# First input rows loaded whole instead of as even and odd halves, with the opening order that goes with it

## The chip, the cores and the metric

The kernel runs on one core of a Trainium2 chip. The metric is the time of one execution on the device in microseconds (us), the median of several runs. The kernel is written against the engines themselves: TensorE (PE in the profile) multiplies, VectorE (DVE) and ScalarE (ACT) do elementwise work and empty the accumulators, GpSimd (POOL) does little, and SyncE (SP) issues nearly all the DMA transfers.

## What is computed

Two convolutions of five taps with stride two over time, each with a gelu, and then a joint of every time step with eight label vectors:

```python
# x (2, 4000, 512), w1, w2 (5, 512, 512), g (2, 8, 512), w_f, w_g, w_o (512, 512), all bf16
h = zeros_like(x)
for i in range(5):
    h = h + einsum("btc,cd->btd", pad(x)[:, i:i+T, :], w1[i])
h = gelu(h)[:, ::2, :]                       # 2000 steps
f = zeros_like(h)
for i in range(5):
    f = f + einsum("btc,cd->btd", pad(h)[:, i:i+T1, :], w2[i])
f = gelu(f)[:, ::2, :]                       # 1000 steps
fe = einsum("btd,de->bte", f, w_f)
ge = einsum("bud,de->bue", g, w_g)
j = tanh(fe[:, :, None, :] + ge[:, None, :, :])
return einsum("btud,dv->btuv", j, w_o)       # (2, 1000, 8, 512)
```

## The kernel before: what the change touches

The program is first written down as a list of operations with what they read and write. A list scheduler with a simple model of durations then fixes the order of the operations of each engine; TensorE and SyncE keep the written order where they are pinned, VectorE, ScalarE and GpSimd are reordered by it. Semaphore waits are derived from that order. So a small edit at the start can change the order of the other engines far behind it.

The convolutions are computed by phases of time (row number modulo 4), with sums and differences of inputs and of weights in place of some of the products. The first tile of `x` (1024 rows, in two blocks of 512 called xr0 and xr1) is loaded with rows in the partitions and transposed by TensorE against an identity; all later tiles come through transposing DMAs. The even rows of a group of four are phases 0 and 2, the odd rows 1 and 3. Here each block is loaded in two transfers, even rows first:

```python
        def load_xr(rt, pp):
            dst = xr[rt][pp::2].map(lambda a: a.rearrange("p r k c -> p r (k c)"))
            src = x[1, 4 * P * rt:4 * P * (rt + 1), :].rearrange("(p r) c -> p r c", r=4)[:, pp::2, :]
            return pl.dma("sp", lambda e: e.dma_start(dst.ap, src), (), (dst,), nbytes=262144)
...
        came = [load_xr(rt, 0) for rt in range(2)]
        act(warm[0:1], warm[1:2], ACT.Gelu_apprx_tanh)
        # w1[i], 512 KB each; `after`: issued when the named earlier transfer has landed
        def load_w1(i, after=None):
            o = load_w("sp", w1_sb[i], w1[i].rearrange("(k c) d -> c k d", c=P))
            if after is not None:
                o.after.append(after.idx)
            return o

        came.append(load_w1(0))
        came += [load_xr(rt, 1) for rt in range(2)]
        for i in (4, 1, 3, 2):
            came.append(load_w1(i, came[-3]))
        for ph in (2, 3, 1, 0):
            load_x(0, ph, 272, 528)
```

`came[-3]` is the third last transfer issued so far: it holds each weight back until an earlier transfer has landed.

TensorE first multiplies zeros (`NWARM = 7` matmuls of 512 columns) while nothing has arrived. Then `turn(pp)` transposes the even (`pp` 0) or odd (`pp` 1) rows of both blocks and copies them from the accumulator into `xs[0]`:

```python
        def warm_mm(n):
            z, zz = zero[0:P], zero[:]
            for i in range(n):
                o = ps.cols((3, 1)[i % 2] * NT, NT)
                mm(o, [(z, zz)], True, True)

        warm_mm(NWARM)
        psb = ps.h[:, :].bitcast(BF16)
        def turn(pp):
            for rt in range(2):
                bk = (1, 3)[rt] if pp else 4 + rt
                pv = View(psb[:, bk * 1024:(bk + 1) * 1024].rearrange("p (r k c) -> p r k c", r=2, k=NK), np.array([bk]), True)

                def fn(e, rt=rt, pv=pv):
                    for r in range(2):
                        for k in range(NK):
                            ins = e.transpose(pv.ap[:, r, k, :], xr[rt].h[:, 2 * r + pp, k, :], ident.h[:, :])
                    return ins
                pl.op("pe", fn, (xr[rt][pp::2], ident[:]), (pv,), 0.6)
                o = xs[0][pp::2, :, 16 + rt * P:16 + (rt + 1) * P]
                if rt:
                    act(o, pv, ACT.Copy)
                else:
                    pl.op("dve", lambda e, o=o, pv=pv: e.tensor_copy(out=o.ap, in_=pv.ap), (pv,), (o,), vec_cost(o, (pv,)))

```

The opening order. `direct(i)` is tap i for the first 128 output channels (8 products of 252 columns); `filt3(w)` is one combined tap for the three other channel groups (12 products). `t0.shift` (ScalarE) and `t0.xf` (VectorE) make the sums and differences of inputs, `w1sum13` and `w1sums` (VectorE, with halvings on ScalarE) those of weights, into `w1_t`, called w_t in the profile:

```python
        turn(0)
        t0.xf("a0")
        t0.shift("a3")
        t0.xf("a3")
        direct(0)
        filt3("a0")
        turn(1)
        t0.shift("b1")
        for w in ("b1", "b3", "a1", "a2"):
            t0.xf(w)
        w1sum13()
        w1sums(2, "s")
        w1sums(1, "s")
        direct(4)
        filt3("a3")
        direct(1)
        direct(3)
        filt3("b1", "b3")
        direct(2)
        pl.pin = ("pe",)

...     # inputs of the second tile; the "+" and "-" halves of the weight sums
        filt3("b2")
        for m in base0:
            filt(m, "a1", "a2")
        t0.gelu(0, ps.pair(0, 256, NA))
```

The tap 2 weight is also halved in place by ScalarE (`w1_sb[2]`, within `w1sum13`), and later in the program the difference `w_b = w1[1] - w1[3]` is made by VectorE and scaled by ScalarE. It is needed much later, and the scheduler decides where it stands.

Of the kernel before, what the change touches and what calls it, by code (L numbers as in the profile page):

```python
# [11 lines left out]
P = 128  # L12
# [297 lines left out]
def bass_standalone__seq2seq_rnn_t_joint__speech_kernel(  # L310
# [30 lines left out]
    NSLOT = 12  # L341
    BU = B * U
    NT = 512
    NWARM = 7
    START = (0, 334, 667, 1000)

    with ExitStack() as es:
        BASE = 16512

        def at(name, shape, dtype, offset):  # L350
            return Buf(nc, name, shape, dtype, BASE + offset)
# [12 lines left out]
        xr = [at(f"xr{i}", [4, NK, P], BF16, H[1] + i * 4096) for i in range(2)]  # L364
# [13 lines left out]
        ident = at("ident", [P], BF16, small + 1408)  # L378
# [13 lines left out]
        pl = Plan(nc)  # L392
# [3 lines left out]
        def vec_cost(o, ins, fast=True):  # L396
            bf = fast and all(not v.psum and v.ap.dtype == BF16 for v in (o,) + tuple(ins))
            return o.ap.free_size() * (0.52e-3 if bf else 1.04e-3) + 0.065
# [8 lines left out]
        def act(o, i, func, scale=1.0, bias=None, cost=None):  # L407
            rd = (i,) if bias is None else (i, bias)
            pl.op("act", lambda e: e.activation(o.ap, i.ap, func, scale=scale,  # L409
                                                bias=0.0 if bias is None else bias.ap), rd, (o,),  # L410
                  cost or o.ap.free_size() * 0.83e-3 + 0.13)

        def mm(o, pairs, start, stop, check=True):

            def fn(e):
                for n, (l, r) in enumerate(pairs):
                    ins = e.matmul(o.ap, lhsT=l.ap, rhs=r.ap, start=start and n == 0,  # L417
                                   stop=stop and n == len(pairs) - 1, skip_group_check=not check)
                return ins
            pl.op("pe", fn, [v for pr in pairs for v in pr], (o,), len(pairs) * max(o.ap.free_size() / 2400 + 0.0025, 0.1))  # L420
# [13 lines left out]
        def load_w(eng, dst, src):  # L434
            return pl.dma(eng, lambda e: e.dma_start(dst.ap, src), (), (dst,))

        def load_xr(rt, pp):
            dst = xr[rt][pp::2].map(lambda a: a.rearrange("p r k c -> p r (k c)"))
            src = x[1, 4 * P * rt:4 * P * (rt + 1), :].rearrange("(p r) c -> p r c", r=4)[:, pp::2, :]
            return pl.dma("sp", lambda e: e.dma_start(dst.ap, src), (), (dst,), nbytes=262144)  # L440

        def load_x(s, ph, lo, hi):

# [4 lines left out]
            pl.dma("sp", lambda e: e.dma_start_transpose(out=dst.ap, in_=src), (), (dst,),  # L448
                   nbytes=(hi - lo) * D * 2, rate=180e3)

        came = [load_xr(rt, 0) for rt in range(2)]
        act(warm[0:1], warm[1:2], ACT.Gelu_apprx_tanh)

        def load_w1(i, after=None):
# [3 lines that stand above are left out]
            return o  # L458

        came.append(load_w1(0))  # L460
        came += [load_xr(rt, 1) for rt in range(2)]
        for i in (4, 1, 3, 2):
            came.append(load_w1(i, came[-3]))
        for ph in (2, 3, 1, 0):
            load_x(0, ph, 272, 528)
# [29 lines left out]
# [5 lines that stand above are left out]

        warm_mm(NWARM)
        psb = ps.h[:, :].bitcast(BF16)
        def turn(pp):
            for rt in range(2):
                bk = (1, 3)[rt] if pp else 4 + rt
                pv = View(psb[:, bk * 1024:(bk + 1) * 1024].rearrange("p (r k c) -> p r k c", r=2, k=NK), np.array([bk]), True)

                def fn(e, rt=rt, pv=pv):
                    for r in range(2):
                        for k in range(NK):  # L510
                            ins = e.transpose(pv.ap[:, r, k, :], xr[rt].h[:, 2 * r + pp, k, :], ident.h[:, :])
                    return ins
                pl.op("pe", fn, (xr[rt][pp::2], ident[:]), (pv,), 0.6)
                o = xs[0][pp::2, :, 16 + rt * P:16 + (rt + 1) * P]
                if rt:
                    act(o, pv, ACT.Copy)
                else:
                    pl.op("dve", lambda e, o=o, pv=pv: e.tensor_copy(out=o.ap, in_=pv.ap), (pv,), (o,), vec_cost(o, (pv,)))

        def shift(src, off, dst, c0, n, which):  # L520

            r, d, kind = {"a0": (2, -1, 0), "a3": (0, 1, 2), "b1": (3, -1, 3)}[which]
            act(dst[kind, :, c0:c0 + n], src[r, :, off + d:off + d + n], ACT.Copy)
# [47 lines left out]
        def w1sums(m, part):  # L571


            nm = 2 if m == 2 else 1
            sl = slice(m * P, (m + nm) * P)
            s = ws[m][:]
            if part == "s":
                tt("dve", s, w1_sb[0, :, sl], w1_sb[4, :, sl], add)
            elif part == "+":
                stt("dve", w1_t[2, :, sl], s, 0.5, w1_sb[2, :, sl], add)  # L580
            else:
                stt("dve", w1_t[0, :, sl], s, 0.5, w1_sb[2, :, sl], sub)
# [286 lines left out]
        t0, t1 = tiles[0:2]  # L869
# [3 lines left out]
        def direct(i):  # L873
            for m in (0,):
                for s in range(2):
                    r, d = tap_at[i][s]
                    mm(ps.cols(m * NT + 256 * s, NA),
                       [(w1_sb[i, k, m * P:(m + 1) * P], xs[0][r, k, 16 + d:16 + d + NA]) for k in range(NK)],
                       i == 0 and s == 0, i == 2, False)
# [3 lines left out]
        def filt(m, *which):  # L883
            A = base0[m]
            C = A + NT
            for w in which:
                o = {"a0": A, "b1": A, "b3": A + NA, "a3": A + NA, "b2": C, "a1": C, "a2": C + NA}[w]
                t0.product(w, m, o, w in ("a0", "b2"))

        def filt3(*which):  # L890
            for w in which:
                for m in base0:
                    filt(m, w)

        turn(0)
        t0.xf("a0")
        t0.shift("a3")
        t0.xf("a3")
        direct(0)
        filt3("a0")  # L900
        turn(1)
        t0.shift("b1")
        for w in ("b1", "b3", "a1", "a2"):
            t0.xf(w)
        w1sum13()
        w1sums(2, "s")
        w1sums(1, "s")
        direct(4)
        filt3("a3")
        direct(1)  # L910
        direct(3)
        filt3("b1", "b3")
        direct(2)
        pl.pin = ("pe",)

# [225 lines left out]
```

## Time and profile before

| | us |
|---|---|
| median of 3 runs | 272.36 |
| lowest and highest | 271.94, 273.29 |
| span of the profiled run | 270.1 |
| TensorE busy | 261.5 |
| VectorE busy | 200.9 |
| ScalarE busy | 181.1 |

The profile is of one execution. Each engine's busy time is the time in which it had an instruction running; a weight load of TensorE (PEld) lies beside the products and is counted apart. In a timeline each line is a run of like instructions: start and duration in us, engine, source line, operation, the tile written and the tile read, the count, and in brackets the idle time of the engine ahead of it with what ended it. The lines named L404, L409 and L417 are helpers that record every elementwise operation of VectorE, every activation and every matmul, so a group is told by its tiles, not by its line. L511 is the transposes, L518 a copy out of the accumulator, L585 a scalar-tensor-tensor operation of VectorE.

The transfers of the program, of which those into xr and w_sb matter here, by size and median time from issue to landing:

| transfer | count | KB each | us to landing |
|---|---|---|---|
| xr from x | 4 | 256 | 4.8 |
| w_sb from w1 and w2 | 10 | 512 | 5.7 |
| xs from x, transposing | 8 | | 4.7 |

### The profile page before, as it was taken

The numbers are of one execution on the slowest core, as the hardware profiler recorded it, in microseconds if no ns is written. First come the engines' busy times: TensorE is split into PE (matmuls) and PEld (weight loads), VectorE is DVE, ScalarE is ACT, GpSimd is POOL, SyncE is SP. The second block draws the span as 40 slices with busy tenths as digits, with TensorE's granted clock in tenths as the row PEclk, the third lists the DMA queues.
The fourth block names the chain that finished last, engine by engine and source line by source line (L and its number), as shares of the span: only waits on it lengthen the run. The fifth ranks groups of instructions, "written<-read, shape, count | busy, mean of one in ns | idle before, by whom it ended". The sixth has DMA issues, their size and how long they took to land.

```text
span 270.1 us, 4333 instructions
## 1 busy us (share of the span) xinstructions
PE 261.5 (97%) x1579; PEld 152.7 (57%) x1579; DVE 200.9 (74%) x362; ACT 181.1 (67%) x302; POOL 6.8 (3%) x20
## 2 busy tenths in 40 slices
PE   6898999999999999999999999999999999999995
PEld 3696765446666556666566545555665444444442
DVE  1389999999999999996233999844345667656664
ACT  2356989995365999667636668738447695959720
POOL 1000003210000000000000000000000000000000
PEclk9799999999999999999999999999999999999999
DMA  5799992969996022111111113321101353454444
GB/s 174 265 239 213 277 283 55 205 117 189 252 177 123 2 78 78 61 38 61 61 39 58 61 59 108 130 77 58 61 19 59 130 164 117 159 190 157 146 148 135
DMA packets 57506, 33.91 MB, mean 126 GB/s; under 512 B 31614, under 2 KB 57486, under 8 KB 57486
## 3 DMA queue, kind: packets, MB, share of 16 engines
q1 hardware_dynamic: 55230, 31.49, 42.9%
q0 software_dynamic: 2112, 2.10, 4.5%
q8 instruction: 12, 0.20, 0.3%
q14 instruction: 8, 0.07, 0.1%
q10 hardware_dynamic: 144, 0.07, 0.1%
HBM read 7.86 MB, written 16.38 MB: 90 GB/s over the span
## 4 chain that ended last, share of the span: by engine, by line
PE 87%; DMA 5%; DVE 3%; ACT 2%; issue 1%; SPq 0%; ACTq 0%
PE acc L417 87%; DMA w_sb<-in_w_dram 5%; ACT jT L409 1%; DVE w_t L585 1%; DVE feT L985 1%; DVE ws L404 1%; SPq L440 0%; DVE zx L404 0%; DVE w_t L404 0%; ACT w_sb L409 0%; DVE row L734 0%; ACT feT L409 0%; ACT fT L409 0%; ACT ost L409 0%; ACTq L271 0%
## 5 line engine op out<-in xcount | busy, mean ns | idle before, releaser
L417 PE MATMUL acc<-wo_sb,jT 128*128 128x512 bf16 (+1 forms) x504 | 114.9, 377 | 0.7 <-ACT jT L409 0.7
L1033 DVE CAST ost<-acc 128x512 bf16<-128x512 f32 (+1 forms) x95 | 64.8, 686 | 37.7 <-PE acc L417 37.7
L409 ACT ACTIVATE jT<-feT,geT 128x1000 bf16<-128x1000 f32 (+16 forms) x100 | 76.6, 820 | 13.3 <-PE acc L417 10.2
L417 PEld LDWEIGHTS acc<-wo_sb,jT 128*128 128x128 bf16 x504 | 49.2, 98 | 53.5 <-ACT jT L409 1.0
L409 ACT ACTIVATE ost<-acc 128x512 bf16<-128x512 f32 (+1 forms) x31 | 18.1, 583 | 16.4 <-PE acc L417 16.0
L417 PE MATMUL acc<-xt,w_sb 128*128 128x252 bf16 (+1 forms) x144 | 24.6, 317 | 0.0
L409 ACT ACTIVATE sd<-acc 128x334 f32<-128x334 f32 (+1 forms) x32 | 13.9, 445 | 11.0 <-PE acc L417 10.9
L409 ACT ACTIVATE hT<-acc 128x334 bf16<-128x334 f32 (+3 forms) x33 | 15.1, 466 | 8.1 <-PE acc L417 7.9
L417 PE MATMUL acc<-row,w_sb 128*128 128x334 bf16 (+1 forms) x112 | 20.5, 305 | 0.0
L417 PEld LDWEIGHTS acc<-xt,w_sb 128*128 128x128 bf16 x144 | 14.6, 102 | 7.5 <-DVE xt L404 0.3
L417 PE MATMUL acc<-zx,w_sb 128*128 128x334 bf16 (+1 forms) x96 | 17.6, 305 | 0.0
L404 DVE TENSOR_TENSOR sd<-sd 128x334 f32<-128x334 f32 (+1 forms) x16 | 8.0, 502 | 10.4 <-ACT sd L409 10.3
L417 PE MATMUL acc<-row,w_t 128*128 128x334 bf16 (+1 forms) x80 | 14.6, 305 | 0.0
L417 PE MATMUL acc<-xs,w_t 128*128 128x252 bf16 (+1 forms) x76 | 14.0, 314 | 0.4 <-issue 0.4
L417 PEld LDWEIGHTS acc<-row,w_sb 128*128 128x128 bf16 x112 | 10.9, 98 | 6.1
L417 PE MATMUL acc<-fT,wf_sb 128*128 128x333 bf16 (+1 forms) x96 | 14.0, 305 | 0.2 <-ACT fT L409 0.2
L417 PE MATMUL acc<-xs,w_sb 128*128 128x252 bf16 (+1 forms) x72 | 11.5, 296 | 1.7 <-DMA w_sb<-in_w_dram 1.7
L409 ACT ACTIVATE fT<-acc 128x334 bf16<-128x334 f32 (+1 forms) x16 | 7.1, 445 | 8.2 <-PE acc L417 8.0
L417 PEld LDWEIGHTS acc<-zx,w_sb 128*128 128x128 bf16 x96 | 9.4, 98 | 5.4
L417 PEld LDWEIGHTS acc<-fT,wf_sb 128*128 128x128 bf16 x96 | 9.3, 97 | 4.5 <-ACT fT L409 0.2
L417 PE MATMUL acc<-hT,w_t 128*128 128x334 bf16 x64 | 11.7, 305 | 0.0
L417 PE MATMUL acc<-hT,w_sb 128*128 128x334 bf16 x64 | 11.5, 305 | 0.0
(86 smaller groups left out, 319.0 us busy)
## 6 DMA issues: line engine op xcount, KB each, us to landing
out_dram<-ost SPq DMA_DIRECT2D x109, 128.0 KB, 1.9
w_sb<-in_w_dram SPq DMA_DIRECT2D x10, 512.0 KB, 5.7
xr<-in_x_dram SPq DMA_DIRECT2D x4, 256.0 KB, 4.8
half<-w_sb POOLq DMA_DIRECT2D x2, 512.0 KB, 6.1
half<-w_t POOLq DMA_DIRECT2D x2, 512.0 KB, 5.2
wf_sb<-in_w_f_dram SPq DMA_DIRECT2D x1, 512.0 KB, 7.5
wg_sb<-in_w_g_dram SPq DMA_DIRECT2D x1, 512.0 KB, 4.8
wo_sb<-in_w_o_dram SPq DMA_DIRECT2D x1, 512.0 KB, 5.8
```

What stands on the lines that cost most here:

```text
L404: pl.op(eng, lambda e: e.tensor_tensor(out=o.ap, in0=a.ap, in1=b.ap, op=op), (a, b), (o,), vec_cost(o, (a, b)))
L409: pl.op("act", lambda e: e.activation(o.ap, i.ap, func, scale=scale, bias=0.0 if bias is None else bias.ap), rd, (o,), cost or o.ap.free_s ...
L417: ins = e.matmul(o.ap, lhsT=l.ap, rhs=r.ap, start=start and n == 0, stop=stop and n == len(pairs) - 1, skip_group_check=not check)
L585: pl.op(eng, lambda e: e.scalar_tensor_tensor(out=o.ap, in0=a.ap, scalar=f, in1=b.ap, op0=ALU.mult, op1=op), (a, b), (o,), vec_cost(o, (a, ...
L985: pl.op("dve", lambda e, o=o, v=v: e.tensor_copy(out=o.ap, in_=v.ap), (v,), (o,), 0.47)
L1033: pl.op("dve", lambda e, o=o, v=v: e.tensor_copy(out=o.ap, in_=v.ap), (v,), (o,), vec_cost(o, (v,)))
```

## The change

The blocks xr0 and xr1 are each loaded by one transfer of 512 KB, in which a partition's four rows are one run in memory, instead of by two of 256 KB. All transposes then stand together: both blocks' even rows, then both blocks' odd rows, in four accumulator banks, with the even copies on VectorE and the odd ones on ScalarE. Ten warm matmuls instead of seven stand ahead of them. With no half of the input late, the taps follow in the order 0, 1, 3, 4, 2 instead of 0, 4, 1, 3, 2, and the weights are loaded in that order; what each weight waits for moves too, since `came` is shorter. The purpose of the simpler order is fewer transfers and an unbroken run of transposes and products.

The name under which the change came speaks of the list scheduler's constants (a longer tail of accumulating DMAs, a longer hop between engines). The scheduler is the same in both files, so nothing of that is in this difference; its fixed orders follow from the edits below. On VectorE and ScalarE the largest move is that of `w_b` from behind the third tile's input sums to a place ahead of the first weight sums; many neighbours are exchanged later on.

```diff
--- before.py
+++ after.py
@@ -341,7 +341,7 @@
     NSLOT = 12
     BU = B * U
     NT = 512
-    NWARM = 7
+    NWARM = 10
     START = (0, 334, 667, 1000)
 
     with ExitStack() as es:
@@ -434,10 +434,10 @@
         def load_w(eng, dst, src):
             return pl.dma(eng, lambda e: e.dma_start(dst.ap, src), (), (dst,))
 
-        def load_xr(rt, pp):
-            dst = xr[rt][pp::2].map(lambda a: a.rearrange("p r k c -> p r (k c)"))
-            src = x[1, 4 * P * rt:4 * P * (rt + 1), :].rearrange("(p r) c -> p r c", r=4)[:, pp::2, :]
-            return pl.dma("sp", lambda e: e.dma_start(dst.ap, src), (), (dst,), nbytes=262144)
+        def load_xr(rt):
+            dst = xr[rt][:].map(lambda a: a.rearrange("p r k c -> p (r k c)"))
+            src = x[1, 4 * P * rt:4 * P * (rt + 1), :].rearrange("(p r) c -> p (r c)", r=4)
+            return pl.dma("sp", lambda e: e.dma_start(dst.ap, src), (), (dst,))
 
         def load_x(s, ph, lo, hi):
 
@@ -448,7 +448,7 @@
             pl.dma("sp", lambda e: e.dma_start_transpose(out=dst.ap, in_=src), (), (dst,),
                    nbytes=(hi - lo) * D * 2, rate=180e3)
 
-        came = [load_xr(rt, 0) for rt in range(2)]
+        came = [load_xr(rt) for rt in range(2)]
         act(warm[0:1], warm[1:2], ACT.Gelu_apprx_tanh)
 
         def load_w1(i, after=None):
@@ -458,8 +458,7 @@
             return o
 
         came.append(load_w1(0))
-        came += [load_xr(rt, 1) for rt in range(2)]
-        for i in (4, 1, 3, 2):
+        for i in (1, 3, 4, 2):
             came.append(load_w1(i, came[-3]))
         for ph in (2, 3, 1, 0):
             load_x(0, ph, 272, 528)
@@ -500,22 +499,23 @@
 
         warm_mm(NWARM)
         psb = ps.h[:, :].bitcast(BF16)
-        def turn(pp):
+        for pp in range(2):
             for rt in range(2):
-                bk = (1, 3)[rt] if pp else 4 + rt
+                bk = 4 + 2 * pp + rt
                 pv = View(psb[:, bk * 1024:(bk + 1) * 1024].rearrange("p (r k c) -> p r k c", r=2, k=NK), np.array([bk]), True)
 
-                def fn(e, rt=rt, pv=pv):
+                def fn(e, rt=rt, pp=pp, pv=pv):
                     for r in range(2):
                         for k in range(NK):
                             ins = e.transpose(pv.ap[:, r, k, :], xr[rt].h[:, 2 * r + pp, k, :], ident.h[:, :])
                     return ins
-                pl.op("pe", fn, (xr[rt][pp::2], ident[:]), (pv,), 0.6)
+                pl.op("pe", fn, (xr[rt][:], ident[:]), (pv,), 0.8)
                 o = xs[0][pp::2, :, 16 + rt * P:16 + (rt + 1) * P]
-                if rt:
+                if pp:
                     act(o, pv, ACT.Copy)
                 else:
                     pl.op("dve", lambda e, o=o, pv=pv: e.tensor_copy(out=o.ap, in_=pv.ap), (pv,), (o,), vec_cost(o, (pv,)))
+
 
         def shift(src, off, dst, c0, n, which):
 
@@ -892,24 +892,20 @@
                 for m in base0:
                     filt(m, w)
 
-        turn(0)
-        t0.xf("a0")
-        t0.shift("a3")
-        t0.xf("a3")
-        direct(0)
-        filt3("a0")
-        turn(1)
-        t0.shift("b1")
-        for w in ("b1", "b3", "a1", "a2"):
+        for w in ("b1", "a3"):
+            t0.shift(w)
+        for w in ("a0", "a1", "a2", "b3", "b1", "a3"):
             t0.xf(w)
         w1sum13()
         w1sums(2, "s")
         w1sums(1, "s")
-        direct(4)
-        filt3("a3")
+        direct(0)
+        filt3("a0")
         direct(1)
         direct(3)
-        filt3("b1", "b3")
+        filt3("b1")
+        direct(4)
+        filt3("b3", "a3")
         direct(2)
         pl.pin = ("pe",)
```

## Prediction

> **What bounds the kernel now.** I first read the page's busy shares. TensorE has work for 97% of the span at a clock that is full but for one dip, so a change can only gain or lose in the stretches where TensorE waits or runs at half speed.
>
> ```profile
> PE 261.5 (97%) x1579; PEld 152.7 (57%) x1579; DVE 200.9 (74%) x362; ACT 181.1 (67%) x302; POOL 6.8 (3%) x20
> PEclk9799999999999999999999999999999999999999
> ```
>
> The 8.6 us without matmuls, and the dip (second digit of PEclk), lie mostly at the start, where the change is. So the next view is TensorE's timeline of the first 36 us (start, duration, operation, idle time before it).
>
> ```profile
> 1.19 3.17 PE L417 MATMUL acc<-zero 128*128 128x512 bf16 x7 [1.19 <-DVE zero L424]
> 4.15 1.06 PE L511 MATMUL acc<-ident,xr 128*128 128x128 bf16 x8
> 5.64 0.62 PE L511 MATMUL acc<-ident,xr 128*128 128x128 bf16 x8 [0.42 <-DMA xr<-in_x_dram]
> 7.93 1.17 PE L417 MATMUL acc<-xs,w_sb 128*128 128x252 bf16 x8 [1.67 <-DMA w_sb<-in_w_dram]
> 8.89 2.73 PE L417 MATMUL acc<-xt,w_sb 128*128 128x252 bf16 x12
> 11.41 1.39 PE L511 MATMUL acc<-ident,xr 128*128 128x128 bf16 x16
> 12.63 1.03 PE L417 MATMUL acc<-xs,w_sb 128*128 128x252 bf16 x8
> ...
> 22.10 3.20 PE L417 MATMUL acc<-xt,w_t 128*128 128x252 bf16 x24 [0.69 <-DVE w_t L585]
> ```
>
> Read here: the first tap (8 products) waits for its weights until 7.93; the 12 "a0" products take 2.73 us where later groups of 12 take 1.45; the 16 transposes of the odd rows come only at 11.41; and at 22.10 the products wait for the weight sums w_t that VectorE makes. Those 24 take 3.20 us, another such group (16.51) 2.74, so w_t costs 0.69 + 0.46 = 1.15 us in all. They end at 25.30. That is my checkpoint: it is the end of all products of the first tile, the same work in both kernels.
>
> Then the same stretch in slices of 1 us (busy time and count by engine, granted clock, DMA share, GB/s).
>
> ```profile
> 7.00:8.00 1.00, 0.07 (x1) 0.10 (x2) 0.65 (x1) 0.97 (x2) 0.00 (x0) 1.00 0.74 260
> 8.00:9.00 1.00, 1.00 (x9) 0.86 (x9) 0.61 (x2) 0.39 (x1) 0.00 (x0) 0.84 0.21 58
> 9.00:10.00 1.00, 1.00 (x7) 0.71 (x6) 0.11 (x1) 0.00 (x0) 0.00 (x0) 0.50 0.25 77
> 10.00:11.00 1.00, 1.00 (x7) 0.71 (x6) 0.00 (x0) 0.00 (x0) 0.00 (x0) 0.50 1.09 386
> ```
>
> Two things: the clock is 0.50 from about 8.67 to 12.09 (from finer slices), which loses 3.42/2 = 1.7 us; and the DMA queue runs dry from 8 to 10 us (58 and 77 GB/s, then 386), because the next weight load is issued only when the first weight has landed. Last, VectorE's timeline, which says why w_t is late.
>
> ```profile
> 12.39 0.69 DVE L518 COPY xs<-acc 128x1024 bf16<-128x1024 bf16 x1 [3.28 <-PE acc L511]
> ...
> 14.97 0.68 DVE L404 TENSOR_TENSOR xt<-xt,xs 128x1008 bf16<-128x1008 bf16 x1 [1.29 <-ACT xt L409]
> 15.57 1.86 DVE L404 TENSOR_TENSOR xt<-xs 128x1008 bf16<-128x1008 bf16 x3
> 17.35 1.22 DVE L404 TENSOR_TENSOR w_t<-w_sb 128x2048 bf16<-128x2048 bf16 x1
> 18.49 1.82 DVE L404 TENSOR_TENSOR ws<-w_sb 128x1024 f32<-128x1024 bf16 x2
> 20.22 3.56 DVE L585 SCALAR_TENSOR_TENSOR w_t<-ws,w_sb 128x1024 bf16<-128x1024 f32 x4
> ```
>
> VectorE idles 3.28 us for the odd transposes and 1.29 us for the shift made from them, then works without a pause from 14.97 on. So w_t is late because the odd rows are late.
>
> **What the Trainium skill says.** "TensorE: Matmul & The Clock Gate", Part 1: the array's clock is half or full, judged in free-running windows of 3413 ns. The trace agrees: 12.09 - 8.67 = 3.42 us at 0.50; TensorE was busy for some 1.4 us of the 3.4 before it. Its Part 4 says that transposes do not count as busy in the same way; no run here shows that yet. "DMA: Bandwidth & Descriptors", Anatomy of one DMA, puts some 2 us of fixed cost on a transfer, most of it the receipt of the last write (it speaks of GpSimd's path). The trace has the like on SyncE's: issue at 7.70, full rate from 10.0.
>
> **The change, part by part.**
>
> *Loads.* Before, 256 KB had landed at 3.7 us (issue 0.7 plus the shortest landing, 3.0), 512 KB at 5.6 (the end of the second transpose wait), 1 MB at 7.70, 1.25 MB at 8.38, 1.5 MB at 9.0 (SyncE's issues that waited for them). The bytes of the first 1.5 MB are the same after, in another order: whole xr0 lands when 512 KB have, at 5.6; xr1 at 7.7; w1[0] at 9.0. That is an estimate on the late side: there is one issue of 0.6 us fewer ahead of w1[0]'s end, and the runs of a partition are longer. w1[1] is now issued at 5.6 and w1[3] at 7.7, so the dry stretch is filled: at about 350 GB/s (slices 10 to 15 have 347 to 386) a 512 KB weight takes 1.5 us, so w1[1] lands at 10.5, w1[3] 12.0, w1[4] 13.5, w1[2] 15.0 against 16.38 before. The x transposing loads behind it start some 1.5 us earlier too.
>
> *TensorE's opening.* Ten warm matmuls of 0.427 us end at 1.19 + 4.3 = 5.5, all within the wait for xr0, so three more cost nothing. Eight transposes 5.6 to 6.2, idle to 7.7, then 24 more at 0.62 per 8: 9.6. w1[0] and VectorE's copy (8.35 + 0.7) are there by then, so the first tap starts at 9.6 instead of 7.93: 1.7 us later. But the odd transposes are behind it. From there at full speed (0.107 us a product): 8 + 12 + 16 + 12 + 8 + 24 + 8 + 12 = 100 products, 10.7 us, to 20.3, each weight in time (w1[3] is needed at 12.6, w1[4] at 14.8, w1[2] at 18.2). Then the 24 on w_t: 2.6 us, to 22.9.
>
> *VectorE and ScalarE.* Odd copies now run on ScalarE (1.02 each): 9.0 to 11.05; its shift for b1 to 12.1. VectorE: copy to 9.1, a0, a1, a2 by 10.9 (0.6 each), b3 to 11.65, b1 to 12.7. New here is w_b = w1[1] - w1[3], 1.15 us, which stood at 40.14 before: to 13.9. Then a3 14.5, w_t 15.6, the three ws (1.15 + 0.6 + 0.6) 18.0, the four scalar-tensor-tensor 18.0 to 21.6, against 20.22 to 23.78 before. ScalarE's scaling of w_b (1.9 us) and of w1[2] (1.4 us) end at 17.2, ahead of 18.0. So w_t is 2.2 us earlier though w_b stands ahead of it, and the last part of it (21.6) meets the product that needs it (about 21.7).
>
> *Clock.* If TensorE's gap of 1.5 us (6.2 to 7.7), against 1.67 + 0.42 before, still brings a half-speed window at the same phase, it hits work only from 9.6 to 12.09 and costs 1.25 us: 24.2. If the fuller window (2.0 of 3.4 us busy against 1.4) keeps the clock up: 22.9. Against 25.3 that is -1.1 or -2.4; I give each half, -1.7.
>
> *Later.* From 25 to 82 us TensorE does not wait, so the lead is carried; the order changes there merely exchange neighbours. At 82 to 93 it waits about 1.2 us on fT and jT, and an engine may not follow the full lead. I carry 85%: -1.5 us. 272.36 - 1.5 = 270.9.
>
> **The rivals.**
> (1) *The later first tap is what counts.* TensorE is 97% busy, and 1.7 us of start are lost. With the half-speed window kept, the end of a0 with all transposes is at 13.0 against 12.63 before: +0.4, and if w_t then is not earlier (xr1 or w1[3] a microsecond later than I think), nothing pays it back: 272.8 to 273.8. For it: the split in pieces was plainly made to start early. Against: VectorE's idle 3.28 and 1.29 us.
> (2) *Transposes do not keep the clock up.* Then the stretch from 5.5 to 9.6 counts as idle; half speed may last beyond 12.1 by a second window, another 1.7 us: 24.2 + 1.7 = 25.9, so 273.0. Against: the 12.09 recovery came after a window that held mainly products, and after 9.6 there are only products.
> (3) *The lead is swallowed* at 82 to 93 us, where TensorE waits for ScalarE and VectorE: about 272.4. Against: these waits follow from TensorE's own output, so they shift with it; and VectorE has w_b already behind it.
>
> **Range and chances.** About 60% for the reasoned gain (269.8 to 271.4), 15% for (3), 25% for (1) and (2), and the runs before differ by 1.3 us. So 270.9, range 269.5 to 273.2. Two per cent is 5.4 us, more than all of the start's waits together, so within 2% is almost sure.
>
> **What would show it.** Right: xr1's transposes end near 9.6 or earlier; GB/s stays over 250 from 3 to 15 us; w_t's wait before the 24 products under 0.3 us; these end before 24.3; the lead is still there at 82 us. Wrong: a w_t wait of over 0.7 us, a half clock after 12.5, the checkpoint at 25 or later, or a new wait of TensorE over 1 us between 25 and 95.

## The result, and the profile after

| | before | after |
|---|---|---|
| median, us | 272.26 | 267.88 |
| lowest and highest, us | 271.94, 273.29 | 267.51, 268.31 |
| span of the profiled run, us | 270.1 | 266.0 |

The ratio is 0.9833, 95% interval 0.9803 to 0.9863: 4.4 us faster, where 1.5 were predicted, and below the predicted range. In a second comparison it was 267.51 against 271.90 us, 0.9871 (0.9840 to 0.9903).

First the page: busy shares and the granted clock.

```profile
PE 260.5 (98%) x1582; PEld 152.1 (57%) x1582; DVE 200.9 (76%) x362; ACT 181.2 (68%) x302; POOL 6.9 (3%) x20
PEclk9999999999999999999999999999999999999999
```

VectorE and ScalarE do the same work to 0.1 us. The dip of the clock is gone (what the row does not tell of the first microseconds comes with the experiments on the clock), and TensorE is without matmuls for 5.5 us instead of 8.6. Its timeline of the start (start, duration, operation, idle time before):

```profile
1.19 4.45 PE L417 MATMUL acc<-zero 128*128 128x512 bf16 x10 [1.19 <-DVE zero L424]
5.43 2.21 PE L510 MATMUL acc<-ident,xr 128*128 128x128 bf16 x32
7.68 1.04 PE L417 MATMUL acc<-xs,w_sb 128*128 128x252 bf16 x8
8.56 1.45 PE L417 MATMUL acc<-xt,w_sb 128*128 128x252 bf16 x12
...
17.17 1.45 PE L417 MATMUL acc<-xs,w_t 128*128 128x252 bf16 x12
18.56 2.75 PE L417 MATMUL acc<-xt,w_t 128*128 128x252 bf16 x24
```

There is no bracket after the first line: from 1.19 to the checkpoint the view shows no wait of TensorE for a transfer or an input. (In the profile of the second comparison it waits once, 0.44 us for xr1.) All 32 transposes follow the warm matmuls, tap 0 starts at 7.68 (before: 7.93), the a0 products take 1.45 us instead of 2.73, and nothing waits for w_t. The checkpoint of the prediction, the end of the 24 products on w_t, is at 18.56 + 2.75 = 21.31 instead of 25.30: 4.0 us. That is the whole gain in the spans (270.1 - 266.0 = 4.1), and it is carried: TensorE's 48 products on fT start at 78.96 instead of 82.95, its first products on jT at 88.69 instead of 92.87.

The loads, in slices of 1 us (TensorE, its weight loads, VectorE, ScalarE, GpSimd busy; then clock, DMA share, GB/s):

```profile
4.00:5.00 1.00, 1.00 (x3) 0.30 (x2) 0.00 (x0) 0.00 (x0) 0.00 (x0) 1.00 1.01 411
5.00:6.00 1.00, 1.00 (x8) 0.72 (x7) 0.00 (x0) 0.00 (x0) 0.00 (x0) 1.00 1.05 375
6.00:7.00 1.00, 1.00 (x21) 1.00 (x20) 0.66 (x2) 0.00 (x0) 0.00 (x0) 1.00 1.06 365
```

The kernel before had moved less in the first two of these slices:

```profile
4.00:5.00 1.00, 1.00 (x9) 0.79 (x7) 0.00 (x0) 0.00 (x0) 0.00 (x0) 1.00 0.92 194
5.00:6.00 1.00, 0.58 (x9) 0.37 (x8) 0.69 (x1) 0.00 (x0) 0.00 (x0) 1.00 0.85 272
```

From 8 to 10 us, where it moved only 58 and 77 GB/s, the changed kernel moves 347 and 335. SyncE's queue shows the landings, since each weight load is issued when an earlier transfer has landed. Its lines of four narrow windows (issue time, duration):

```profile
4.48 0.38 SPq L435 DMA_DIRECT2D w_sb<-in_w_dram  x1
5.77 0.37 SPq L435 DMA_DIRECT2D w_sb<-in_w_dram  x1
7.27 0.37 SPq L435 DMA_DIRECT2D w_sb<-in_w_dram  x1
8.76 0.37 SPq L435 DMA_DIRECT2D w_sb<-in_w_dram  x1
```

So xr0 has landed at 4.48 at the latest, xr1 at 5.77, w1[0] at 7.27, w1[1] at 8.76. Last, VectorE:

```profile
6.34 1.29 DVE L517 COPY xs<-acc 128x1024 bf16<-128x1024 bf16 x2 [5.20 <-PE acc L510]
7.66 2.46 DVE L404 TENSOR_TENSOR xt<-xs 128x1008 bf16<-128x1008 bf16 x4
10.28 0.69 DVE L404 TENSOR_TENSOR xt<-xt,xs 128x1008 bf16<-128x1008 bf16 x1 [0.15 <-ACT xt L409]
10.88 1.22 DVE L404 TENSOR_TENSOR w_b<-w_sb 128x2048 bf16<-128x2048 bf16 x1
...
16.08 3.55 DVE L585 SCALAR_TENSOR_TENSOR w_t<-ws,w_sb 128x512 bf16<-128x512 f32 x4
```

From 6.34 until past the end of these lines it shows a single pause, of 0.15 us. The four scalar-tensor-tensor operations start at 16.08 instead of 20.22, although w_b (1.15 us) now stands ahead of them.

### The profile page after: what moved, and what is told of

Read it like the earlier page. It is cut to its first block, busy times and chain, and to the rows that moved or that the text cites. A ratio compares the mean times of both kernels' runs of the same rounds, so it can differ in the third digit from the quotient of the medians.

```text
span 266.0 us, 4332 instructions
## 1 busy us (share of the span) xinstructions
PE 260.5 (98%) x1582; PEld 152.1 (57%) x1582; DVE 200.9 (76%) x362; ACT 181.2 (68%) x302; POOL 6.9 (3%) x20
## 4 chain that ended last, share of the span: by engine, by line
PE 80%; DVE 14%; ACT 3%; issue 2%; DVEq 0%; ACTq 0%
PE acc L417 79%; DVE wide L404 2%; DVE r L585 2%; DVE r32b L585 2%; ACT w_t L409 1%; DVE ws L585 1%; DVE hT L404 1%; ACT jT L409 1%; DVE feT L981 1%; PE acc L510 1%; DVE sd L585 1%; DVE wide L734 1%; DVE row L585 1%; DVE row L734 1%; DVE acc L585 1%
## 5 line engine op out<-in xcount | busy, mean ns | idle before, releaser
L417 PE MATMUL acc<-xt,w_sb 128*128 128x252 bf16 (+1 forms) x144 | 23.5, 305 | 0.0
L417 PEld LDWEIGHTS acc<-xt,w_sb 128*128 128x128 bf16 x144 | 14.0, 98 | 7.0 <-DVE xt L404 0.3
```

## Experiments: is it the loads or the order?

Theory A was that the form of the loads does it, rival B that the order does, rival C that the number of transfers does. In the first three kernels all orders of all engines are those of the changed kernel; only the two transfers of x differ. The first cuts each by even and odd rows (`d` and `src` are the block by partition, row and channel; the operation waits for both pieces):

```diff
-            return pl.dma("sp", lambda e: e.dma_start(dst.ap, src), (), (dst,))
...
+            def fn(e):
+                e.dma_start(d[:, 0::2, :], src[:, 0::2, :]).then_inc(sem[0], 16)
+                return e.dma_start(d[:, 1::2, :], src[:, 1::2, :])
+            return pl.dma("sp", fn, (), (dst,), sem)
```

> The changed kernel with each 512 KB block of x fetched again as two transfers of 256 KB by even and odd rows (runs of 1 KB), all orders of all engines as changed. Theory A (the loads' form decides: the short strided runs are slow): xr1 lands near 7.5 us instead of 5.8, TensorE idles over 1 us between the warm matmuls and the products, the clock falls to half again, time 269.5 to 271.5. Rival B (the gain lies in the order of transposes and taps and in the queue that no longer runs dry): within 0.4 us of the changed kernel's 267.9. Rival C (the number of transfers decides, not the runs): slower by about 1 us, and as slow with runs of 4 KB.

Measured: 270.85 us, 0.9954 of before (0.9930 to 0.9978). TensorE's timeline of this kernel:

```profile
5.34 0.61 PE L516 MATMUL acc<-ident,xr 128*128 128x128 bf16 x8
8.52 2.65 PE L516 MATMUL acc<-ident,xr 128*128 128x128 bf16 x24 [2.57 <-DMA xr<-in_x_dram]
10.97 1.57 PE L417 MATMUL acc<-xs,w_sb 128*128 128x252 bf16 x8
```

The wait of 2.57 us and a half clock (0.50 from 9 to 12 us) are back; 14 of the 22 runs show a mean clock of 0.994 or less. Most of the gain is lost with the old form of the loads, so rival B fails as a sole cause.

The second takes neighbouring rows, `d[:, 0:2, :]` and `d[:, 2:4, :]` (runs of 2 KB); the third halves of the partitions, `d[0:64]` and `d[64:128]` (runs of 4 KB).

> The same with pieces of neighbouring rows (0 and 1, 2 and 3: runs of 2 KB). Theory A: between the 1 KB and the 4 KB form, 268 to 269.5. Rival B: 267.9. Rival C: as the other two forms in pieces, about 269.

> The same with pieces by partitions (0 to 63, 64 to 127: runs of 4 KB as in the whole transfer). Theory A: as the changed kernel, 267.7 to 268.3. Rival B: 267.9 too. Rival C: about 1 us slower, as the 1 KB form.

Measured: 269.00 us, 0.9913 (0.9879 to 0.9948), and 270.45 us, 0.9962 (0.9940 to 0.9984). The second block arrives at 6.4 us with the 2 KB pieces and at 8.0 with the 4 KB pieces, where whole transfers bring it at 5.8. Theory A had put the third kernel at 267.7 to 268.3: run length alone is not the reason. Pieces are slower in all three forms, as rival C says, but not equally so.

The fourth is the kernel before with whole blocks of x: its order, its seven warm matmuls.

```diff
-        came = [load_xr(rt, 0) for rt in range(2)]
+        came = [load_xr(rt) for rt in range(2)]
...
-        came += [load_xr(rt, 1) for rt in range(2)]
```

> The kernel before, with its order of transposes and taps (even transposes, tap 0, a0, then odd transposes) and seven warm matmuls, but the blocks of x fetched whole; VectorE and ScalarE are ordered anew by the scheduler. Theory A (loads decide): the landings of the changed kernel (xr1 near 5.8, first weight near 7.3), no half clock, time 268 to 269.5. Rival B (order decides): the loads help little, VectorE still waits for the odd transposes and w_t is late, 270.5 to 272.

Measured: 271.43 us, 0.9972 (0.9947 to 0.9997). Both blocks come as in the changed kernel (389 and 395 GB/s from 3 to 5 us, xr1 landed by 5.69), and the first weight 0.6 us later than there (by 7.83, not 7.27). Yet nearly nothing is gained, because the order does not use them (the view ends at 24 us, within the last group):

```profile
8.06 1.71 PE L417 MATMUL acc<-xs,w_sb 128*128 128x252 bf16 x8 [1.72 <-DMA w_sb<-in_w_dram]
9.56 2.47 PE L417 MATMUL acc<-xt,w_sb 128*128 128x252 bf16 x12
11.87 1.06 PE L510 MATMUL acc<-ident,xr 128*128 128x128 bf16 x16
...
22.23 2.02 PE L417 MATMUL acc<-xt,w_t 128*128 128x252 bf16 x13 [0.69 <-DVE w_t L584]
```

TensorE idles with the odd rows already in the buffer, and w_t is late as before. In this run the clock falls too, as in 6 of the 22. Theory A fails as well: neither half of the change works alone. The clock does not decide this: among the runs whose mean clock is 0.998 or more, the medians are 270.79 us (before), 269.45 (first experiment) and 270.56 (fourth), where the changed kernel has 267.5 to 267.9.

## Experiments: which part of the order?

The next kernel is the fourth with one call moved.

```diff
         turn(0)
+        turn(1)
         t0.xf("a0")
...
         filt3("a0")
-        turn(1)
         t0.shift("b1")
```

> As the old order with whole blocks (271.43), but the odd transposes stand straight behind the even ones; taps still in the order 0, 4, 1, 3, 2, seven warm matmuls. Theory D (whole loads and odd transposes at once belong together: only then does TensorE work through from the warm matmuls on, and VectorE has all phases early): half clock gone or short, w_t wait under 0.3 us, 268 to 269. Rival E (the new order of taps or the ten warm matmuls do it): 270 to 271.5, half clock still there.

Measured: 268.22 us, 0.9904 (0.9869 to 0.9939). The changed kernel ran beside it:

> The changed kernel unaltered, to stand on the same chip as the next three: 267.5 to 268.5 by either theory.

Measured: 267.51 us, 0.9871 (0.9840 to 0.9903). Moving the odd transposes forward takes the old order from 271.43 to 268.22 us, and no run shows a fall of the clock. Theory D holds: whole blocks and all transposes at once belong together. (The scheduler orders VectorE and ScalarE anew with this move, so it is the move together with the order that it brings.) What makes up the 0.7 us that remain is argued and not shown: the order of taps and weights, with what the scheduler makes of it. The profile is of the longest of the six runs (269.47 us). It keeps a w_t wait of 0.32 us, because ScalarE halves w1[2] only at 15.48, when that last weight has landed, and VectorE waits for it until 17.06; and 1.02 us of idle time at 24.96 that no wait explains.

Ten warm matmuls instead of seven were then tested in the changed kernel (`NWARM = 7`):

> The changed kernel with seven warm matmuls instead of ten, orders of all engines the same. Theory D: the warm matmuls only fill TensorE's wait for the first block (landed at 4.4 us, seven end at about 4.2), so the time stays within 0.4 us of 267.5 where the clock is granted, and the odd run loses up to 1.7 us to a half-speed window: median 267.4 to 268.2. Rival W (the ten warm matmuls are what keeps the clock up): half clock in the profile or a median over 268.8.

Measured: 267.79 us, 0.9865 (0.9833 to 0.9897). Rival W fails: the three additional warm matmuls neither cost nor bring anything that these runs resolve. With seven, the transposes of the first block start at 4.44 us and the others wait for the second block until 5.70, so the three stand in time in which TensorE would wait anyway.

## Experiments: the clock and the dry queue

The kernel before, with its idle time filled (seven products of zeros, in two banks that nothing holds yet; orders kept):

```diff
         turn(0)
+        for i in range(7):
+            zo, zz = ps.cols((3, 1)[i % 2] * NT, NT), zero[:]
+            pl.op("pe", lambda e, ...: e.matmul(zo.ap, lhsT=zero.h[:, 0:P], rhs=zz.ap, ...), (zz,), (zo,), 0.0)
         t0.xf("a0")
```

> The kernel before with seven more multiplications of zeros in TensorE's wait between the even transposes and tap 0; all other orders the same. It measures the clock alone. Theory D: no half clock at 8.7 to 12.1, which returns up to 1.7 us less what w_t then holds back: 270.5 to 271.3, with the w_t wait still there or longer. Rival F (the half clock is the whole difference): 268 to 269. Rival G (products of zeros do not hold the clock, or the clock is not what costs): 272.

Measured: 270.46 us, 0.9966 (0.9947 to 0.9985). None of its 23 runs shows a fall of the clock (all means are 0.998 or more), and 21 of them lie between 269.87 and 270.97 us. So filling the hole brings 1.4 us of the 4.4, and not the whole. The profile is of the longest run, 272.15 us:

```profile
6.84 3.06 PE L898 MATMUL acc<-zero 128*128 128x512 bf16 x7
...
22.25 3.20 PE L417 MATMUL acc<-xt,w_t 128*128 128x252 bf16 x24 [0.70 <-DVE w_t L585]
```

The w_t wait is still there. The first line shows something else: these products of 512 columns start 427 ns apart, where others of this size start 216 ns apart later on (eight in 1.90 us at 88.69 in the changed kernel). So TensorE is at half speed here until about 9.65 us (an estimate from the last of them, which takes 337 ns), though the clock column says 1.00, because the record of the clock begins with its first rise. Every profile of this case begins at half speed in this way (warm matmuls 427 ns apart), and the rise comes at another time in each: at 3.97 us in the second profile of the changed kernel, 5.26 in the kernel before, 5.95 in the first profile of the changed kernel. A mean clock of 1.000 says only that the clock did not fall again.

The runs of the kernel before fall into groups that agree with the 1.4 us. Of the 35 beside this one, 19 have a mean clock of 0.994 and took 271.68 to 272.56 us (median 272.20); of the 15 with 1.000, twelve took 269.35 to 271.55 and three over 273; one with 0.987 took 273.54. Of the 64 beside the first four experiments, 28 have 0.994 (median 272.03); of the 34 with 1.000, 21 took 269.76 to 271.59 and 13 took 272.72 to 273.45; two with 0.987 took 273.5. A rise as late as in the profile above would fit these long runs at 1.000, but none of them was profiled, so their cause is not shown. The changed kernel's six runs all have 0.998 or more and lie between 267.40 and 267.71. The Trainium skill, "TensorE: Matmul & The Clock Gate", Part 1, says that the window is free-running and does not start with the kernel, so that the same kernel meets it at different phases. That agrees with the rises above and with these groups: the kernel before, with a hole in TensorE's start, draws a lot in each run; the changed kernel does not.

How large a hole matters can be read from the profiles. In the three that show a fall it comes 3.41 us after the rise, and the clock is back after another 3.41. In the 3.41 us from rise to fall TensorE was busy for 1.37 us (before, from 5.26), 0.85 (first experiment, from 5.24) and 1.19 (fourth, from 4.82). In the 3.41 us behind the rise it was busy for 1.84 us in the third experiment (from 6.08), 1.98 in the kernel of the next experiment (from 6.09) and 2.00 with seven warm matmuls (from 5.07), and no fall followed. The 1.84 us of the third were transposes but for the last 0.1. If transposes did not count, it would stand at 0.1, below all three that fell; so they do hold the clock here, other than the prediction's note from the skill had it.

The dry stretch of the queue, filled in the kernel before (w1[4], w1[1] and w1[3] are issued two landings earlier; w1[2] waits for w1[4] as before and is issued at 10.74 instead of 11.86):

```diff
-        for i in (4, 1, 3, 2):
-            came.append(load_w1(i, came[-3]))
+        for i, j in ((4, 0), (1, 1), (3, 2), (2, 5)):
+            came.append(load_w1(i, came[j]))
```

> The kernel before with each later weight load issued two landings earlier (w1[4] when the even rows of xr0 have landed, and so on), so that the DMA queue does not run dry at 8 to 10 us; orders of all engines the same. Theory D: w_t is held back by the odd transposes and VectorE, not by the transfers, so 271.8 to 272.4, or worse where weights then compete with the odd rows. Rival H (the dry queue is what made w_t late): 270.5 to 271.3, the w_t wait gone.

Measured: 271.92 us beside 271.90, 0.9996 (0.9963 to 1.0029). The slices from 8 to 10 us now move 351 and 384 GB/s, and nothing comes of it: the w_t wait is still there, in a profile of a run whose clock did not fall.

```profile
7.78 1.02 PE L417 MATMUL acc<-xs,w_sb 128*128 128x252 bf16 x8 [1.43 <-DMA w_sb<-in_w_dram]
...
9.93 1.06 PE L511 MATMUL acc<-ident,xr 128*128 128x128 bf16 x16
10.82 1.03 PE L417 MATMUL acc<-xs,w_sb 128*128 128x252 bf16 x8
...
20.29 3.20 PE L417 MATMUL acc<-xt,w_t 128*128 128x252 bf16 x24 [0.69 <-DVE w_t L585]
```

Rival H fails: in the old order VectorE and the odd rows hold w_t back, not the weights (VectorE works without a pause from 13.15 until w_t is made). This profile also lets the 4.0 us of the checkpoint be taken apart. From the start of tap 0 to the checkpoint it takes 23.49 - 7.78 = 15.7 us, the kernel before 25.30 - 7.93 = 17.4, the changed kernel 21.31 - 7.68 = 13.6. So the half clock is 1.7 us. The other 2.1 are the odd transposes, which no longer stand between the products (9.93 to 10.82, 0.9 us), and w_t (the wait of 0.69 and the 0.46 by which its 24 products take longer). The last 0.25 us is tap 0, which starts earlier.

## Experiments: why whole blocks come sooner

The changed kernel with the rows of a partition written 32 bytes apart, so that a whole transfer consists of runs of 1 KB (orders kept):

```diff
-        xr = [at(f"xr{i}", [4, NK, P], BF16, H[1] + i * 4096) for i in range(2)]
+        xr = [at(f"xr{i}", [4, 528], BF16, X[2] + i * 4224) for i in range(2)]
```

> The changed kernel with the same two whole transfers of 512 KB, but the rows of a partition written 32 bytes apart (another place for the buffer), so that each transfer consists of runs of 1 KB; all orders the same. Theory R (the runs decide how fast x comes): the second block lands near 7 us instead of 5.7 and the time is 269 to 271. Rival N (the number of transfers and of their issues ahead of w1[0] decides): landings and time as in the changed kernel, 267.4 to 268.2.

Measured: 268.59 us, 0.9894 (0.9865 to 0.9923). SyncE's lines of narrow windows:

```profile
0.74 1.37 SPq L440 DMA_DIRECT2D xr<-in_x_dram  x2
...
5.20 0.39 SPq L435 DMA_DIRECT2D w_sb<-in_w_dram  x1
6.60 0.37 SPq L435 DMA_DIRECT2D w_sb<-in_w_dram  x1
```

The landings are 0.7 to 0.8 us later than in the profile after. Short runs cost this once: the two issues take 1.37 us instead of 0.87, little moves before 3 us (62 GB/s from 2 to 3, against 217), and from there the rate is nearly the same (334, 383, 340, 357 GB/s in four slices, against 344, 411, 375, 365). So the runs explain a part: the landing and the time lie between the two expectations.

Two more asked whether every transfer has a price. One cuts the four later weights into pieces of 256 KB, the other joins both blocks of x in one transfer of 1 MB.

> The changed kernel with the weights w1[1], w1[3], w1[4] and w1[2] each fetched in two transfers of 256 KB, x whole, orders of all engines the same. If every transfer costs time on the DMA engines (theory P): the rate between 8 and 12 us falls from about 350 GB/s to 260 to 300, w1[2] is issued 1 us later or more, and the time rises by 0 to 0.6 us as TensorE still has its weights. If only the pieces of x are slow (rival X): 340 GB/s and more, issue of w1[2] within 0.3 us of 8.7.

> The changed kernel with both blocks of x in one transfer of 1 MB, still runs of 4 KB; VectorE, ScalarE and GpSimd are ordered anew. Theory P: x has landed whole at about 5.5 us and w1[0] at 6.9 (0.3 us earlier each), the transposes of the first block start later. Rival X: x at 5.7, w1[0] at 7.2. Time 267.3 to 268.5 by either.

Measured: 268.39 us, 0.9885 (0.9824 to 0.9946), and 269.61 us, 0.9929 (0.9905 to 0.9953). With weights in pieces the slices from 8 to 11 us still move 349 to 353 GB/s, the slice from 7 to 8 only 206, and w1[2] is issued at 9.41 instead of 8.76: between the two theories. With x in one transfer, x has landed at 5.78 and w1[0] at 7.20, no sooner than with two. Tap 0 starts at 8.03, and the weights come later (101 GB/s from 7 to 8 us; w1[1], issued at 5.78 instead of 4.48, lands by 9.75 instead of 8.76). VectorE, in its new order, waits 0.78 us for a weight ahead of sums of inputs for which TensorE then waits 0.8 us. Why the pieces of x move more slowly (239 to 269 GB/s from 4 to 7 us with runs of 1 KB, 168 to 274 with halves of the partitions) stays open.

## Experiments: a better version?

Transposes block by block (the two loops over `rt` and `pp` exchanged), and in the second kernel the second block issued by ScalarE:

> The changed kernel with the transposes block by block (both phases of the first block, then of the second) instead of phase by phase; VectorE and ScalarE ordered anew by the scheduler. After the second block has landed 16 transposes are left instead of 24, so tap 0 could start 0.4 to 0.5 us earlier, unless w1[0] (7.27 us) is then what it waits for: 267.0 to 267.5. If the landing of w1[0] or another order of VectorE takes it back: 267.5 to 268.3.

> As the last, and the second block issued by ScalarE instead of SyncE, beside the first, so that w1[0] is issued 0.4 us earlier too. If the issue on SyncE delays the start: second block and w1[0] land up to 0.4 us earlier, 266.7 to 267.3. If the transfers are bound by the bytes (365 to 411 GB/s in the changed kernel): landings unchanged, 267.2 to 268.

Measured: 268.62 us, 0.9903 (0.9873 to 0.9933), and 269.56 us, 0.9928 (0.9903 to 0.9954). In the first, tap 0 starts at 7.26, no sooner than in the changed kernel of the second comparison, since it now waits for a copy of VectorE; and the scheduler gives VectorE another order, with new waits of TensorE behind it (0.9 us for a sum of VectorE, 0.2 for xt). In the second, ScalarE's issue brings no earlier landing (both blocks 4.9 to 5.1 us after their issues), and TensorE waits 1.7 us for a copy of ScalarE. Neither beats the changed kernel.

## Why the prediction was wrong, point by point

**Direction and mechanism** were right. The odd rows held VectorE, VectorE held w_t; the half clock hit products; the checkpoint moved and nothing behind it took the lead back. Of the signs of being right one was missed: the rate fell to 189 and 114 GB/s from 13 to 15 us, at no cost to TensorE.

**The loads: the term that failed.** The prediction took the landings of the old pieces as a schedule of bytes: xr1 at 7.7, w1[0] at 9.0, called on the late side. Measured were 5.77 and 7.27. A landing was treated as a matter of bytes alone, but the old rate of 194 to 272 GB/s belonged to transfers in pieces with runs of 1 KB; the whole blocks moved 344 to 411. Hence the transposes ended at 5.43 + 2.21 = 7.64, where the prediction said 9.6: 2.0 us. The predicted checkpoint without a half clock, 22.9, less 2.0 is 20.9, against 21.3 measured; the 0.4 between them is in the products, which took a little longer than 0.107 us each (7.68 to 21.31 for 124 of them). The prediction had itself named the two reasons for an earlier landing (one issue fewer, longer runs) and gave them no number. What the experiments show of the reasons: runs of 1 KB cost 0.7 to 0.8 us by themselves, and with x in pieces it had landed 0.6 to 2.7 us later; why pieces are slower stays open.

**The clock** was a coin toss in the prediction (1.25 us or nothing). For the hole that it reckoned with, that was fair: the third experiment has a wait of 1.57 us there, and the clock fell in 11 of its 22 runs. But with xr1 at 5.77 there is no such hole, and no run of the changed kernel shows a fall. That is 0.65 us over the mean that was used, and it follows from the loads as well. Not foreseen was that the runs of the kernel before are themselves a mixture: its median holds some 1.4 us of half clock. The reading "a clock that is full but for one dip" was wrong for the first 5.26 us, which are at half speed too, but both kernels begin so.

**VectorE and w_t.** Predicted 18.0 for the first scalar-tensor-tensor and no wait; measured 16.08 and no wait. Of the 1.9 us, 1.4 are there when the first xt starts (7.66 where 9.1 was predicted), which is the loads again; another 0.3 is a shorter wait for ScalarE's shift (0.15 us instead of 0.45). That w_b stands ahead at no cost was right.

**The dry queue** was named beside the clock as one of two things to see, though no term of the sum stood for it. Filling it in the old order changed nothing.

**Carried on.** 85% was assumed, 100% was measured (4.0 us at the checkpoint, 4.1 in the spans). That is 0.25 us of the 1.7 that were to be carried, a discount without a reason in the trace.

**The rivals.** (1) the later first tap: it was not later (7.68 against 7.93). (2) a second half-speed window, because transposes do not keep the clock up: no run of the changed kernel shows a fall, and in the third experiment 1.84 us of nearly nothing but transposes kept the clock up. (3) the lead swallowed: not seen.

In sum, 2.3 us were missing at the checkpoint (1.7 predicted on the mean, 4.0 measured): 1.6 from the landings directly and 0.65 from the clock. The 15% that was held back come on top (0.25), and 0.3 is the distance between the medians (4.4) and the two profiled runs (4.1). The range was too narrow on the fast side: it let the landings vary upwards, and not by the 2 us that the old pieces might have been slow.

## What to carry to other kernels

A landing time read from one form of transfer does not hold for another: size and run length set the start and the rate, so give a change of form its own term and its own range. An early start of the bound engine is worth little if it leaves a hole behind it; the hole cost TensorE its clock here in about half the runs, and the late half of the data held up the engine that prepares the weights. A clock column that starts at 1.00 is no evidence of full speed at the start: compare the spacing of equal matmuls. And one profile may be of an untypical run: look where its time lies among the others. Two parts of a change can each be worth almost nothing alone (271.4 and 270.9 us here) and 4 us together, so undo them one at a time and also do them one at a time.

## What the runs showed of the hardware

- Two issues of a 512 KB load by SyncE took 0.87 us with runs of 4 KB and 1.37 us with runs of 1 KB, and everything landed 0.7 to 0.8 us later; the rate once under way was nearly the same.
- The same 1 MB of x in four transfers of 256 KB had landed at about 6.4 us (runs of 2 KB), 8.0 (half the partitions each, runs of 4 KB) and 8.5 (runs of 1 KB), against 5.8 in two whole transfers.
- A half-speed window followed 3.41 us in which TensorE had been busy for 0.85, 1.19 or 1.37 us (three profiles); once the clock had risen, none followed 3.41 us with 1.84 us busy or more, even where nearly all of it was transposes.
- Every profile began at half speed, until 3.97 to 6.30 us and once until about 9.65, which the clock column does not show.
- 24 transposes in a row took 1.51 us at the full clock: they start 56 ns apart, and 107 ns apart at half speed.
